# Another order for the first eleven stretches of an attention kernel, rows spread by GpSimd, and three moves in its routed path

## The chip, the cores and the metric

The kernel runs on one core of a Trainium2 chip. The metric is the device time of one execution in microseconds (us); the median of several executions is taken. The core has five engines, each with its own instruction queue: TensorE (PE, matmuls), VectorE (DVE), ScalarE (ACT), GpSimd (POOL) and SyncE (SP, which here only issues transfers). They meet through semaphores. A transfer (DMA) is issued by an engine's queue and carried out by sixteen DMA engines that all queues share.

## What is computed

The reference, cut to what matters:

```python
def reference(A_x, A_k_cache, A_v_cache, A_wq, A_wo, B_x, B_w_r, B_w_gate, B_w_up, B_w_down):
    xn = _layernorm(A_x)                        # 2048 tokens x 640
    s = _A_ref(xn, A_k_cache, A_v_cache, A_wq, A_wo)
    g = _silu(_B_ref(xn, B_w_r, B_w_gate, B_w_up, B_w_down))
    return A_x + s * g

def _A_ref(x, k_cache, v_cache, wq, wo):        # 32 heads of 192, the last 512 keys
    q = (x @ wq).reshape(B, Sq, 32, 192)
    p = _softmax(q . k * 192 ** -0.5)
    return (p . v).reshape(B, Sq, 32 * 192) @ wo

def _B_ref(x, w_r, w_gate, w_up, w_down):       # two tokens of 2048 pass an expert
    r = x @ w_r
    idx = jnp.argsort(-r)[:, :2]
    y = (_silu(x[idx] @ w_gate) * (x[idx] @ w_up)) @ w_down      # F = 1536
    return x.at[idx].add(y * _sigmoid(r[idx]))
```

The two functions are shortened here to their arithmetic. All inputs and the output are bfloat16. I call the first the attention and the second the routed path.

## The kernel before

The 2048 tokens are 16 blocks of 128. The attention works on 256 units, each two heads by one block. Four units, a pair of heads by 512 tokens, make a step (64 steps), and three units make a stretch (86 of them, the first two with two units). The kernel is software-pipelined by stretch: in stretch j PE makes the scores of its units, some q for later steps, then the product with v of stretch j - 1 and some of the output projection.

The instructions of every engine stand in the order in which the program issues them; no scheduler reorders them. Tokens write this order out, and `first` (L647) turns each into instructions. For stretches 0 to 10 the list `FIRST` (L843) is written by hand (`J0 = 11`, L842); from 11 on, `stretch(j)` (L813) makes the tokens by rule. The order of the tokens decides the order on each engine alone; engines wait for each other's results. The tokens, with n a block or unit, j a stretch, i a step:

- `x`, `k`, `v`, `wq`, `wo`: a load of tokens, keys, values or weights, on SP's queue, or on ACT's with the suffix `.a`.
- `bn` (DVE, L163) or `as` (ACT, L233 and L234, with one instruction of POOL, L235): the statistics of a block. `pw.lo.hi`: the reciprocal roots for blocks lo to hi - 1, four instructions of POOL (L211 to L214). `ap.n`: the normalization into `xn`, on ACT (`a`, L246), POOL (`g`, L249) or DVE (`v`, L251). `sx`, `ex`, `sq`, `rc`: function tables of ACT and the roots of blocks 0 and 1.
- `turn.n`: five transposes of `xn` on PE and a copy (L255). `xT.lo.hi`: the same for two blocks by a transposing DMA on SP (L262).
- `kt`: the transposes of the first pair's keys on PE (L265); `kT.p`: those of a later pair by DMA on SP (L119).
- `q.i.c`: five matmuls (L301) for a third of a step's q, and `qe.i.c` its way out of PSUM (L289 to L293), on ACT unless the token ends in `.v`; in the first step, split in two halves by two further numbers, it runs on ACT in every case.
- `S.j`: six scores of 512 keys, each of two matmuls (L315, then L322). `M.n.h`: a row maximum on DVE (L330). `E.n.h`: an exponential on ACT (L337). `P.n`: the transpose of the exponentials by DMA on SP, into `pT` (L342). `R.j`: reciprocals of the sums (L346).
- `O.n`: eight matmuls with v (L356); `OO` does two units. `Oe.n`: their scaling on DVE or ACT (L371, L369). `T.j`: the transpose of the result by DMA on SP (L377).
- `W.w`: the output projection of one block and two steps (L404); `We.w`: its way out into `s_acc` (L416, L418).
- `B.j.slot`: what the background has in stretch j, at its start (slot 0), behind the exponentials (1), in the middle (2) or at its end (3). The list of the background is written with `at(unit, slot, ...)` (L729). In the part that `FIRST` covers all of these are empty; `B.12.3` is the first of the routed path.

PSUM has eight banks: `ps_f` two ("f": q, a single `O`, the transposes), `ps_p` six ("p": scores, `OO`, the projection). A bank is handed to the next user in the order in which the former users gave theirs back.

The routed path is background work. `m_open` (L437) comes at unit 36 (stretch 12): it loads the router's row w_r onto all 128 partitions and makes constants on POOL. `m_r` (DVE) makes the router's score of each block from unit 39 on, `m_rows` and `m_top` (L476) turn them and find the two best of each block; these 64 numbers go to a buffer in DRAM (`c_d`) and come back on all partitions (L488 to L491). `m_sel` (L493), `m_tok` and `m_own` find the two best of all and gather their rows from the input by an indirect DMA; `m_norm` (L536) normalizes them, with the reciprocal root on POOL, `m_scale` and `m_xsT` follow. `m_mul` (L564) makes the expert's gate and up products of a third of F, `m_hT` turns the result, `m_down` (L602) multiplies by w_down, and its two rows go through another buffer in DRAM (`y_d`, L610 to L614) onto all partitions. `m_add` (L616) adds them to half of `xn` on POOL, from unit 147 on. `m_tanh` (L625, ACT) and `m_gate` (L629, DVE) make the silu of a block, from unit 186 on, one block every second unit.

Of the kernel before, what the change touches and what calls it, by code (L numbers as in the profile page):

```python
# [21 lines left out]
def kernel(ctx, tc, A_x, A_k_cache, A_v_cache, A_wq, A_wo, B_x, B_w_r, B_w_gate, B_w_up, B_w_down, out):  # L22
# [414 lines left out]
    def m_open():  # L437
# [6 lines left out]
        nc.gpsimd.dma_start(out=M["wr"], in_=B_w_r.partition_broadcast(P))  # L444
# [31 lines left out]
    def m_top():  # L476
# [12 lines left out]
        nc.gpsimd.dma_start(out=c_d, in_=cand)  # L489
# [412 lines left out]
```

## Time and profile before

| | before |
|---|---|
| median of 3 runs | 803.88 us |
| lowest, highest | 802.24, 804.67 us |
| the profiled execution | 803.23 us |
| its span, first to last instruction | 801.5 us |
| mean granted clock of TensorE | 0.996 |

Busy time by part of the span, in us:

| stretch of time | PE | DVE | ACT | POOL | granted clock |
|---|---|---|---|---|---|
| 0 to 7 | 5.55 | 3.25 | 2.32 | 0.55 | 1.00 |
| 7 to 17.6 | 8.39 | 8.59 | 9.49 | 1.56 | 1.00 |
| 17.6 to 24.1 | 4.42 | 6.13 | 6.43 | 2.88 | 1.00 |
| 24.1 to 70 | 43.42 | 34.16 | 35.09 | 11.23 | 0.96 |
| 70 to 780 | 709.05 | 558.04 | 425.92 | 148.60 | 1.00 |
| 780 to 801.5 | 14.72 | 15.00 | 2.78 | 9.96 | 0.94 |

All times inside an execution count from the start of its span. A group of instructions in the profile reads: line, engine, operation, output and inputs by the program's names, shape, count, busy time, mean of one. An engine's name with "q" is a queue of transfers, "PEld" the load of weights into TensorE. In brackets stands the idle time ahead of an instruction and what ended it. A list of waits reads: who waited for whom, total us, count, and longest.

### The profile page before, as it was taken

How to read it: one execution, taken by the hardware profiler on the slowest of the kernel's cores; microseconds unless marked ns; L12 is line 12 of the kernel's file. 1: busy time of each engine (PE TensorE's matmuls, PEld its weight loads, DVE VectorE, ACT ScalarE, POOL GpSimd, SP SyncE). 2: the span in 40 equal slices, each digit the busy share in tenths (PEclk: the TensorE clock that was granted, in tenths of full speed). 3: DMA queues.
4: the chain of work that ended last, by engine and by line, in shares of the span. 5: the costliest groups of instructions: out<-in, count | busy, mean ns of one | idle time of the engine just before them, and what ended most of it. 6: DMA issues, size and time to landing. Idle time of an engine off the chain costs nothing. (4 is left out here: it accounts for less than half of the span.)

```text
span 801.5 us, 15649 instructions
## 1 busy us (share of the span) xinstructions
PE 785.5 (98%) x5748; PEld 481.5 (60%) x5748; DVE 625.2 (78%) x1243; ACT 482.0 (60%) x1303; POOL 174.8 (22%) x194
## 2 busy tenths in 40 slices
PE   8899999999999999999999999999999999999996
PEld 4456556665666566666556665666566665566565
DVE  6876668989888777777777777777788887877786
ACT  7886676556655556655565556565566865565560
POOL 1330000000000000000001999920000000265954
PEclk9999999999999999999999999999999999999999
DMA  8999998789979999699997999879997889997994
GB/s 239 192 207 218 201 189 143 136 183 193 177 137 201 205 206 206 128 216 199 215 219 139 164 188 201 143 140 173 201 165 137 160 177 202 168 195 154 166 176 117
DMA packets 453389, 143.80 MB, mean 179 GB/s; under 512 B 422350, under 2 KB 452816, under 8 KB 453312
## 3 DMA queue, kind: packets, MB, share of 16 engines
q1 hardware_dynamic: 449872, 138.76, 92.8%
q0 software_dynamic: 928, 2.50, 1.1%
q10 hardware_dynamic: 2512, 1.54, 0.7%
q8 instruction: 45, 0.74, 0.4%
q14 instruction: 32, 0.26, 0.1%
...
## 5 line engine op out<-in xcount | busy, mean ns | idle before, releaser
L337 ACT ACTIVATE pexp<-sc,nm 128x512 bf16<-128x512 f32 x512 | 348.4, 696 | 292.5 <-issue 242.5
L330 DVE TENSOR_REDUCE nm<-sc 128x1 f32<-128x512 f32 x512 | 314.7, 681 | 78.7 <-PE sc L322 78.7
L301 PE MATMUL q_ps<-xnT,wq_p 128*128 128x512 bf16 (+1 forms) x975 | 226.3, 376 | 3.2 <-ACT pexp L337 0.8
L404 PE MATMUL w_ps<-wo_g,oT 128*128 128x320 bf16 x1542 | 223.2, 299 | 0.5 <-DMA oT<-o_sb 0.5
L404 PEld LDWEIGHTS <-oT 128*128 128x128 bf16 x1542 | 150.2, 98 | 71.0 <-DMA oT<-o_sb 0.8
L356 PE MATMUL o_ps<-v_sb,pT 128*128 128x192 bf16 x2048 | 185.2, 246 | 2.4 <-DMA pT<-pexp 1.3
L356 PEld LDWEIGHTS <-pT 128*128 128x128 bf16 x2048 | 170.9, 98 | 18.1 <-issue 4.9
L301 PEld LDWEIGHTS <-wq_p 128*128 128x128 bf16 x975 | 88.4, 98 | 127.1 <-issue 37.5
L371 DVE TENSOR_TENSOR o_sb<-o_ps,lsum 128x384 bf16<-128x384 f32 x239 | 131.6, 557 | 40.2 <-PE o_ps L356 22.0
L315 PE MATMUL sc<-kT,qT 128*128 128x512 bf16 x512 | 126.1, 382 | 0.9 <-DMA kT<-k_raw 0.9
L418 DVE TENSOR_TENSOR s_acc<-s_acc,w_ps 128x320 f32<-128x320 f32 x192 | 92.1, 483 | 32.2 <-PE w_ps L404 32.2
L337 ACT ACTIVATION_READ_ACCUMULATOR pexp<-sc,nm 128x1 f32 x512 | 109.8, 214 | 0.0
L293 ACT ACTIVATE qT<-q_ps 128x512 bf16<-128x512 f32 (+1 forms) x179 | 98.8, 606 | 1.3 <-PE q_ps L301 1.1
L315 PEld LDWEIGHTS <-qT 128*128 128x128 bf16 x512 | 49.0, 98 | 42.7 <-issue 2.1
L322 PE MATMUL sc<-kT,qT 64*128 64x512 bf16 x512 | 70.6, 382 | 0.0
L643 POOL TENSOR_TENSOR s_acc<-s_acc,xn 128x640 f32<-128x640 f32 x16 | 22.5, 1403 | 113.7 <-DVE s_acc L418 113.7
L322 PEld LDWEIGHTS <-qT 64*128 64x128 bf16 x512 | 18.1, 94 | 47.0 <-issue 36.8
L622 POOL TENSOR_TENSOR xn<-xn,yh 128x640 bf16<-128x640 bf16 x32 | 44.7, 1396 | 2.7
...
L644 POOL TENSOR_TENSOR s_acc<-s_acc,x_fin 128x640 f32<-128x640 f32 x16 | 22.4, 1400 | 62.5 <-DMA x_fin<-in_A_x_dram 61.5
L489 POOL DMA_DIRECT2D c_d<-cand x1 | 0.5, 547 | 155.4 <-DVE cand L487 155.4
L621 POOL TENSOR_SCALAR yh<-y_bc,oh 128x640 bf16<-128x640 bf16 x32 | 25.7, 803 | 5.0 <-DMA y_bc<-y_d 3.5
...
## 6 DMA issues: line engine op xcount, KB each, us to landing
...
pT<-pexp SPq DMA_TRANSPOSE x256, 3.7
...
```

What stands on the lines that cost most here:

```text
L293: nc.scalar.activation(out=out, in_=in_, func=ACT.Copy, scale=scale)
L301: nc.tensor.matmul(q_ps, lhsT=wq_of[g * PAIRS + pr][:, dc, c * P:(c + 1) * P], rhs=xnT[:, t5 * 4 + lo:t5 * 4 + hi, dc, :], start=(dc == 0) ...
L315: nc.tensor.matmul(sc_of[n][hh], lhsT=qT_of[i][:, 2 * hh, u * P:(u + 1) * P], rhs=kp[:, :, 2 * hh, :], start=True, stop=False)
L322: nc.tensor.matmul(sc_of[n][hh], lhsT=qT_of[i][hs, 1, u * P:(u + 1) * P], rhs=kp[hs, :, 1, :], start=False, stop=True)
L330: nc.vector.tensor_reduce(out=nm_of[j][:, c:c + 1], in_=sc_of[n][hh], axis=AX.X, op=ALU.max, negate=True)
L337: nc.scalar.activation(out=pe_of[n][:, hh, :], in_=sc_of[n][hh], func=ACT.Exp, bias=nm_of[j][:, c:c + 1], scale=1.0, accum_out=l_of[j][:, ...
L356: nc.tensor.matmul(ps[:, hh, :], lhsT=pT_of[n][:, hh, jj, :], rhs=v_sb[:, hh, jj, :], start=(jj == 0), stop=(jj == NJ - 1))
L371: nc.vector.tensor_tensor(out=osb_of[j][:, m], in0=ps, in1=l_of[j][:, 2 * m:2 * m + 2].unsqueeze(2).to_broadcast([P, 2, Dh]), op=ALU.mult)
L404: nc.tensor.matmul(w_ps, lhsT=oT_of[j][:, stretches[j].index(n), c % 3, :], rhs=wo_of[g][:, c, lo:hi], start=(c == 0), stop=(c == CPG - 1))
L418: nc.vector.tensor_tensor(out=acc, in0=acc, in1=w_ps, op=ALU.add)
L621: nc.gpsimd.tensor_scalar(out=yh, in0=M["y_bc"][:, j, :], scalar1=M["oh"][:, n, j:j + 1], scalar2=0.0, op0=ALU.mult, op1=ALU.add)
L622: nc.gpsimd.tensor_tensor(out=xn[:, n, :], in0=xn[:, n, :], in1=yh, op=ALU.add)
```

## The change

Four things are edited. The hand-written order `FIRST` is replaced: the same work in another sequence, some of it on other engines. Blocks 4 and 14 get their statistics from DVE (`bn`) instead of ACT (`as`). `kT.1` stands ahead of `P.0` and no longer behind it. The normalizations of blocks 5, 7 and 14 go to POOL, of 6 and 15 to DVE, of 8 and 12 to ACT. Five ways out of q, fifteen scalings of o and three of the projection change between DVE and ACT. One load of tokens and two of keys go to ACT's queue, and `wq.1`, `wq.2` and `k.1.0` leave it for SP's.

Three rows (w_r, the candidates, the expert's result) are no longer loaded onto 128 partitions; a short load brings each to one partition, and POOL's `partition_broadcast` spreads it. The candidates and the expert's result no longer pass through DRAM. In the built program this puts six switches of POOL's code library into its queue, one ahead of each broadcast and one ahead of the next instruction of the ordinary kind (in the lines of the new kernel L446, L457, L493, L545, L616, L620). The other switch of the program, near L142, is in both.

`m_mul` moves from slot 2 (middle) to slot 3 (end) of its stretch, and for the first third with its `m_hT` from unit 86 to unit 88, one stretch on. `m_tanh` moves from slot 1 to slot 0, `m_gate` of every even block from slot 3 to slot 2.

The diff, without the lines of `FIRST` for stretches 6 to 10:

```diff
--- before.py
+++ after.py
@@ -441,7 +441,9 @@
         M["s"] = M["stack"].enter_context(tc.tile_pool(name="moe_s", bufs=1))
         M["ws"] = (M["w"], M["s"])
         M["wr"] = M["s"].tile([P, D], BF16, name="wr_bc", tag="t3")
-        nc.gpsimd.dma_start(out=M["wr"], in_=B_w_r.partition_broadcast(P))
+        row = M["s"].tile([1, D], BF16, name="wr_row", tag="t1")
+        nc.gpsimd.dma_start(out=row, in_=B_w_r.rearrange("(o d) -> o d", o=1))
+        nc.gpsimd.partition_broadcast(M["wr"], row)
         M["r"] = M["s"].tile([P, NTB], FP32, name="r_pn")
         M["r_b"] = M["s"].tile([P, P], BF16, name="r_b", tag="turned")
         nc.gpsimd.memset(M["r_b"], 0.0)
@@ -485,10 +487,10 @@
         nc.vector.tensor_copy(out=cand[:, 0, :], in_=top[:, 0:2])
         nc.vector.tensor_copy(out=cand[:, 1, :], in_=loc[:, 0:2])
         nc.vector.tensor_scalar(out=cand[:, 1, :], in0=cand[:, 1, :], scalar1=M["base"][:, 0:1], scalar2=None, op0=ALU.add)
-        c_d = tc.dram_tile([NTB, 2, 2], FP32, name="c_d")
-        nc.gpsimd.dma_start(out=c_d, in_=cand)
+        row = M["s"].tile([1, NTB, 4], FP32, name="cand_row", tag="t2")
+        nc.gpsimd.dma_start(out=row, in_=cand.rearrange("n k c -> n (k c)"))
         M["cand"] = M["w"].tile([P, NTB, 2, 2], FP32, name="cand_bc", tag="w")
-        nc.gpsimd.dma_start(out=M["cand"].rearrange("p n k c -> p (n k c)"), in_=c_d.rearrange("n k c -> (n k c)").partition_broadcast(P))
+        nc.gpsimd.partition_broadcast(M["cand"].rearrange("p n k c -> p (n k c)"), row.rearrange("o n k -> o (n k)"))
 
     def m_sel():
 
@@ -607,11 +609,11 @@
                                  start=(fc == 0), stop=(fc == FC - 1), skip_group_check=True)
         y_sb = M["s"].tile([P, DQ], BF16, name="y_sb", tag="t2")
         nc.vector.tensor_scalar(out=y_sb, in0=y_ps, scalar1=M["sgp"][:, 0:1], scalar2=None, op0=ALU.mult)
-        y_d = tc.dram_tile([2, D], BF16, name="y_d")
+        row = M["s"].tile([1, 2, 4, DQ], BF16, name="y_row", tag="rows")
         for c in range(4):
-            nc.gpsimd.dma_start(out=y_d[:, c * DQ:(c + 1) * DQ], in_=y_sb[32 * c:32 * c + 2, :])
+            nc.gpsimd.dma_start(out=row[:, :, c, :], in_=y_sb[32 * c:32 * c + 2, :])
         M["y_bc"] = M["w"].tile([P, 2, D], BF16, name="y_bc", tag="w")
-        nc.gpsimd.dma_start(out=M["y_bc"], in_=y_d.partition_broadcast(P))
+        nc.gpsimd.partition_broadcast(M["y_bc"].rearrange("p k d -> p (k d)"), row.rearrange("o k c d -> o (k c d)"))
 
     def m_add(n):
         def f():
@@ -759,16 +761,16 @@
     for fb, n0 in enumerate((72, 91, 106)):
         for q in range(2 * DC):
             at(n0 + q, 0, m_ffn_piece(fb, q))
-        at(n0 + 14, 2, m_mul(fb))
-        at(n0 + 14, 3, m_hT(fb))
+        at(n0 + (16, 14, 14)[fb], 3, m_mul(fb))
+        at(n0 + (16, 14, 14)[fb], 3, m_hT(fb))
     for q in range(FC // 2):
         at(121 + 2 * q, 0, m_wd_piece(q))
     at(124, 3, m_sig)
     at(138, 2, m_down)
     for n in range(NTB):
         at(147 + 2 * n, 3, m_add(n))
-        at(186 + 2 * n, 1, lambda n=n: m_tanh(n))
-        at(186 + 2 * n, 3, lambda n=n: m_gate(n))
+        at(186 + 2 * n, 0, lambda n=n: m_tanh(n))
+        at(186 + 2 * n, 2 + n % 2, lambda n=n: m_gate(n))
     at(220, 3, fin_open)
 
 
@@ -841,18 +843,18 @@
 
     J0 = 11
     FIRST = """
-B.3.3 x.0.0.1.a x.0.1.2 k.0.0 bn.0.0 k.0.1.a bn.1.0 x.0.2.3 bn.0.1 sx sq.0.1 wq.0 bn.1.1 sq.1.2 kt.0.a rc.0.1 ap.0.v rc.1.2 kt.1.v x.0.3.4 ap.1.v bn.2.0 turn.0.a turn.1.v q.0.0.0.2 q.0.2.0.2 ex bn.2.1 qe.0.0.v.0.2 k.1.0.a bn.3.0 bn.3.1 qe.0.2.v.0.2 wq.1.a x.1.2.4 q.0.1.0.2 qe.0.1.a.0.2 x.1.0.2 pw.2.4 
-S.0 k.1.1 as.4 ap.2.v ap.3.v turn.2.v turn.3.a M.0.0 q.0.0.2.4 E.0.0 M.1.0 q.0.2.2.4 qe.0.0.v.2.4 E.1.0 bn.7.0 q.0.1.2.4 M.0.1 qe.0.2.v.2.4 v.1 qe.0.1.a.2.4 bn.6.0 B.2.0 bn.7.1 E.0.1 
-S.1 bn.6.1 x.2.0.2 M.1.1 q.1.2 x.2.2.4 as.5 q.1.0 pw.4.8 v.0 M.2.1 E.1.1 qe.1.2.a M.2.0 E.2.0 R.0 M.3.1 E.2.1 as.8 q.1.1 ap.6.g ap.4.v ap.5.v M.3.0 B.3.2 E.3.0 qe.1.0.v P.0 kT.1 bn.11.0 B.3.1 bn.9.0 ap.7.v O.0 qe.1.1.v E.3.1 bn.11.1 P.1 
-S.2 B.3.0 P.2 B.2.1 bn.9.1 xT.4.6 xT.6.8 M.4.0 as.10 P.3 B.4.0 M.5.0 pw.8.12 Oe.0.a M.4.1 O.1 E.5.0 M.5.1 q.2.0 E.5.1 x.3.0.2 Oe.1.v E.4.0 M.6.0 E.6.0 qe.2.0.v T.0 x.3.2.4 E.4.1 P.4 q.2.1 R.1 q.2.2 M.6.1 qe.2.1.v B.2.2 ap.8.g qe.2.2.v E.6.1 ap.9.g O.2 
-S.3 Oe.2.a ap.11.v M.7.0 P.5 M.8.0 M.8.1 as.12 ap.10.g O.3 E.7.0 Oe.3.a P.6 E.8.0 q.3.1 q.3.0 M.9.1 M.9.0 E.8.1 M.7.1 bn.13.0 E.7.1 qe.3.0.v OO.4.5 xT.8.10 R.2 E.9.0 Oe.4.v E.9.1 xT.10.12 qe.3.1.a Oe.5.v q.3.2 qe.3.2.v bn.13.1 P.8 
-S.4 T.1 O.6 as.15 B.2.3 q.4.1 B.7.2 P.7 Oe.6.a M.10.1 P.9 R.3 M.10.0 E.10.0 M.12.0 q.4.0 E.12.0 wo.0.0 M.11.0 wo.0.1 E.10.1 E.11.0 P.10 qe.4.1.v T.2 M.12.1 OO.7.8 M.11.1 E.12.1 qe.4.0.v E.11.1 O.9 Oe.7.v Oe.8.v Oe.9.v as.14 
-S.5 pw.12.16 P.11 q.4.2 M.13.0 E.13.0 M.13.1 P.12 M.14.0 M.14.1 M.15.0 E.14.0 ap.15.g B.5.3 B.4.3 E.14.1 q.5.0 qe.5.0.a E.13.1 M.15.1 qe.4.2.v W.0 B.6.3 ap.14.v E.15.0 OO.10.11 R.4 Oe.10.a E.15.1 T.3 B.5.2 Oe.11.a P.14 O.12 Oe.12.a ap.12.g P.13 We.0.v B.6.1 
...
+x.0.0.1.a x.0.1.2 bn.0.0 x.0.3.4.a bn.0.1 k.0.0 bn.1.0 B.2.0 x.0.2.3 k.0.1.a sq.0.1 wq.0 rc.0.1 sx B.3.3 bn.1.1 ap.0.v x.1.0.2 sq.1.2 rc.1.2 kt.0.a turn.0.a bn.3.0 kt.1.a bn.3.1 ap.1.v turn.1.v bn.2.0 bn.2.1 q.0.0.0.2 x.1.2.4 qe.0.0.v.0.2 q.0.2.0.2 q.0.1.0.2 v.0 qe.0.2.v.0.2 bn.4.0 qe.0.1.v.0.2 
+S.0 bn.4.1 pw.2.4 ex bn.6.0 ap.2.v k.1.0 ap.3.v M.0.0 turn.2.a turn.3.v M.0.1 q.0.0.2.4 wq.1 E.0.0 k.1.1 qe.0.0.v.2.4 q.0.2.2.4 bn.7.0 B.3.0 E.0.1 q.0.1.2.4 qe.0.2.v.2.4 x.2.2.4 bn.7.1 qe.0.1.v.2.4 bn.6.1 M.1.0 x.2.0.2 as.5 M.1.1 pw.4.8 
+S.1 B.3.1 M.2.0 q.1.2 M.3.0 B.4.0 qe.1.2.v M.2.1 v.1 q.1.1 kT.1 E.1.0 q.1.0 P.0 E.1.1 ap.4.v qe.1.1.a M.3.1 ap.6.v E.2.0 qe.1.0.v B.2.2 E.3.0 R.0 ap.5.g P.1 E.3.1 B.5.3 bn.9.0 O.0 ap.7.g E.2.1 as.8 bn.9.1 bn.11.0 Oe.0.v xT.4.6 
+S.2 M.4.0 M.6.0 bn.11.1 M.5.0 as.10 xT.6.8 P.2 E.5.0 O.1 P.3 Oe.1.v E.6.0 M.4.1 pw.8.12 q.2.0 E.4.0 M.5.1 B.3.2 B.5.2 qe.2.0.v q.2.2 x.3.0.2 x.3.2.4 E.4.1 ap.11.v E.5.1 T.0 M.6.1 P.4 qe.2.2.v R.1 q.2.1 qe.2.1.v ap.10.g bn.13.0 E.6.1 P.6 
+S.3 R.2 M.7.0 as.12 O.2 E.7.0 M.8.0 Oe.2.v ap.8.a M.7.1 O.3 Oe.3.v E.7.1 P.5 q.3.1 qe.3.1.a M.8.1 E.8.0 ap.9.g M.9.1 B.4.3 E.8.1 xT.10.12 M.9.0 T.1 q.3.0 E.9.0 q.3.2 OO.4.5 qe.3.0.v E.9.1 qe.3.2.v Oe.4.a as.15 R.3 Oe.5.v 
+S.4 O.6 xT.8.10 P.8 bn.13.1 M.10.0 P.7 Oe.6.a M.11.0 q.4.1 M.12.0 M.10.1 qe.4.1.v B.2.3 P.9 wo.0.0 E.11.0 bn.14.0 bn.14.1 E.12.0 wo.0.1 M.11.1 E.10.0 T.2 E.10.1 B.7.2 E.11.1 M.12.1 E.12.1 OO.7.8 Oe.7.v O.9 P.11 P.10 P.12 Oe.8.v Oe.9.v 
+S.5 q.4.0 pw.12.16 M.14.0 M.13.0 qe.4.0.a ap.15.v R.4 M.13.1 M.15.0 B.2.1 M.14.1 q.5.0 E.13.0 ap.14.g B.6.2 B.6.1 M.15.1 E.13.1 q.4.2 E.14.0 qe.5.0.v W.0 E.14.1 B.10.3 E.15.0 We.0.v OO.10.11 ap.13.g Oe.10.a Oe.11.a qe.4.2.v xT.14.16 E.15.1 
...
     """.split()
 
     for token in FIRST:
```

More of the change, by code (lines that the diff above doesn't have):

```diff
@@ L852 @@
-S.7 Oe.15.v qe.6.0.v M.20.0 q.6.1 B.10.3 M.19.0 M.21.0 qe.6.1.v E.19.0 B.5.1 M.21.1 M.20.1 M.19.1 E.20.0 q.6.2 E.21.0 E.19.1 E.20.1 W.3 O.18 W.4 T.5 wq.2.a v.2 qe.6.2.v E.21.1 We.4.v OO.16.17 k.3.0 R.6 We.3.a Oe.16.v Oe.17.a
-S.8 M.22.0 Oe.18.a M.23.1 E.22.0 B.9.1 P.21 M.22.1 q.7.0 R.7 M.24.1 P.19 M.23.0 P.20 E.22.1 E.23.0 B.7.0 q.7.1 qe.7.0.a k.3.1 qe.7.1.a E.23.1 W.6 M.24.0 W.5 We.6.v E.24.0 wq.3 E.24.1 OO.19.20 B.6.0 P.22 Oe.19.a T.6 We.5.v Oe.20.a B.9.0
-S.9 P.23 M.26.0 kT.3 B.10.1 M.26.1 O.21 Oe.21.v M.25.1 E.26.0 q.8.0 M.25.0 E.26.1 E.25.0 E.25.1 W.7 q.7.2 B.10.2 M.27.0 qe.8.0.a P.24 OO.22.23 E.27.0 M.27.1 qe.7.2.v E.27.1 T.7 P.26 R.8 B.8.1 Oe.22.v Oe.23.a q.8.1 P.25 kT.2 We.7.v
@@ L855 @@
-S.10 M.28.0 M.28.1 M.29.0 qe.8.1.a O.24 R.9 B.8.3 B.8.2 B.9.2 Oe.24.v P.27 E.28.0 v.3 M.30.0 E.28.1 q.9.0 qe.9.0.v E.29.0 M.30.1 E.30.0 OO.25.26 M.29.1 B.10.0 P.28 Oe.25.a q.8.2 E.29.1 B.9.3 E.30.1 O.27 qe.8.2.a Oe.26.a T.8 W.9 P.29 P.30 Oe.27.a W.8 wo.1.1 We.9.a T.9 We.8.a
+x.0.0.1.a x.0.1.2 bn.0.0 x.0.3.4.a bn.0.1 k.0.0 bn.1.0 B.2.0 x.0.2.3 k.0.1.a sq.0.1 wq.0 rc.0.1 sx B.3.3 bn.1.1 ap.0.v x.1.0.2 sq.1.2 rc.1.2 kt.0.a turn.0.a bn.3.0 kt.1.a bn.3.1 ap.1.v turn.1.v bn.2.0 bn.2.1 q.0.0.0.2 x.1.2.4 qe.0.0.v.0.2 q.0.2.0.2 q.0.1.0.2 v.0 qe.0.2.v.0.2 bn.4.0 qe.0.1.v.0.2
@@ new lines @@
+S.6 R.5 T.3 B.6.3 O.12 M.16.0 M.17.0 B.4.1 P.14 ap.12.a q.5.1 Oe.12.v B.7.3 M.17.1 P.13 E.16.0 M.16.1 E.17.0 M.18.1 E.16.1 W.2 B.8.0 qe.5.1.a xT.12.14 M.18.0 E.18.0 P.15 E.18.1 T.4 We.2.v q.5.2 E.17.1 OO.13.14 qe.5.2.v P.16 k.2.0 B.7.1 P.18 Oe.13.v Oe.14.v q.6.0 W.1 B.5.0 O.15 We.1.a qe.6.0.a
+S.7 M.21.0 P.17 Oe.15.a E.21.0 M.19.1 M.19.0 T.5 E.19.0 M.20.0 M.21.1 v.2 q.6.1 B.10.2 wo.1.0 qe.6.1.v k.2.1.a M.20.1 k.3.0.a E.19.1 B.4.2 q.6.2 E.21.1 R.6 E.20.0 W.4 P.21 We.4.a O.18 E.20.1 OO.16.17 Oe.16.v wq.2 P.19 W.3 qe.6.2.v We.3.a Oe.17.v
@@ new lines @@
+S.8 M.22.0 q.7.1 P.20 k.3.1 Oe.18.a M.24.0 E.22.0 M.23.0 M.23.1 M.22.1 E.23.0 q.7.0 E.22.1 E.23.1 W.6 qe.7.0.a M.24.1 W.5 E.24.0 B.9.0 E.24.1 OO.19.20 B.8.1 wq.3 P.23 We.6.v R.7 We.5.a Oe.19.v Oe.20.v B.9.1 P.22 B.5.1 B.10.0
+S.9 B.6.0 qe.7.1.a O.21 M.26.0 Oe.21.v M.26.1 q.8.0 E.26.0 M.25.1 q.7.2 M.25.0 E.26.1 E.25.0 qe.7.2.v E.25.1 M.27.1 M.27.0 E.27.0 W.7 E.27.1 qe.8.0.a We.7.v R.8 P.24 OO.22.23 T.6 q.8.1 Oe.22.a Oe.23.v
+S.10 M.28.1 qe.8.1.a M.28.0 E.28.0 M.29.0 q.9.0 B.7.0 kT.2 P.25 M.29.1 O.24 B.8.3 P.26 B.8.2 P.27 M.30.0 E.28.1 R.9 qe.9.0.v Oe.24.a OO.25.26 T.7 E.29.0 E.29.1 M.30.1 B.9.3 T.8 O.27 q.8.2 P.28 Oe.25.a v.3 wo.1.1 E.30.0 W.8 E.30.1 B.10.1 B.9.2 We.8.a Oe.26.v P.30 P.29 Oe.27.a T.9 qe.8.2.a W.9 kT.3 We.9.a
```

1 line of the change is left out of this document (removed).

## The prediction

> **What bounds the kernel now.** I read the engine totals first, then busy time by stretch, then what TensorE waited for, then its order of work where it waited.
>
> ```profile
> PE 785.5 (98%) x5748; PEld 481.5 (60%) x5748; DVE 625.2 (78%) x1243; ACT 482.0 (60%) x1303; POOL 174.8 (22%) x194
> ```
> ```profile
> core 0: us, PE busy (x) PEld busy (x) DVE busy (x) ACT busy (x) POOL busy (x), PEclk, DMA share, GB/s
> 7.00:10.40 3.40, 2.00 (x24) 1.58 (x22) 2.90 (x8) 2.98 (x5) 0.00 (x0) 1.00 1.09 360
> 20.70:24.10 3.40, 1.46 (x12) 0.90 (x11) 3.40 (x9) 3.37 (x9) 1.18 (x3) 1.00 1.18 142
> 24.10:27.50 3.40, 3.40 (x10) 0.95 (x11) 1.35 (x5) 2.50 (x8) 1.43 (x4) 0.51 1.24 235
> 27.50:70.00 42.50, 40.02 (x279) 22.80 (x275) 32.81 (x63) 32.59 (x91) 9.80 (x25) 1.00 1.07 204
> 70.00:780.00 710.00, 709.05 (x5223) 436.66 (x5222) 558.04 (x1098) 425.92 (x1156) 148.60 (x139) 1.00 0.96 178
> ```
>
> TensorE (PE) is busy 98% of the span. Between 70 and 780 us it idles 710.00 - 709.05 = 0.95 us. All that this change does to the routed path lies there, so no edit to it can gain more than 0.95 us; it can only lose. The loss that can be won back lies before 70 us, and there the other engines are full: from 20.7 to 24.1 VectorE (DVE) and ScalarE (ACT) were busy without a break while PE worked 1.46 of 3.40 us. Right behind it the granted clock is 0.51, once in the run.
>
> ```profile
> PE o_ps L356 <- DVE qT L291: 1.0, 1, 1.0
> PE o_ps L356 <- DMA pT<-pexp: 0.9, 2, 0.8
> ...
> PE w_ps L404 <- DMA oT<-o_sb: 0.5, 1, 0.5
> PE q_ps L301 <- DMA xnT<-xn: 0.4, 1, 0.4
> ```
> ```profile
> 17.59 3.71 PE L301 MATMUL q_ps<-xnT,wq_p 128*128 128x512 bf16 x15
> 22.33 0.82 PE L356 MATMUL o_ps<-v_sb,pT 128*128 128x192 bf16 x8 [1.03 <-DVE qT L291]
> 24.06 2.68 PE L315 MATMUL sc<-kT,qT 128*128 128x512 bf16 x6 [0.91 <-DMA kT<-k_raw]
> 26.68 1.23 PE L322 MATMUL sc<-kT,qT 64*128 64x512 bf16 x6
> 27.84 0.83 PE L356 MATMUL o_ps<-v_sb,pT 128*128 128x192 bf16 x8
> 29.48 0.81 PE L301 MATMUL q_ps<-xnT,wq_p 128*128 128x512 bf16 x3 [0.80 <-ACT pexp L337]
> ...
> 33.43 1.46 PE L315 MATMUL sc<-kT,qT 128*128 128x512 bf16 x6
> 34.82 0.82 PE L322 MATMUL sc<-kT,qT 64*128 64x512 bf16 x6
> 35.58 0.83 PE L356 MATMUL o_ps<-v_sb,pT 128*128 128x192 bf16 x8
> ...
> 71.02 2.33 PE L301 MATMUL q_ps<-xnT,wq_p 128*128 128x512 bf16 x10
> ```
>
> The first view lists waits of the first 130 us, the second PE's work in order of time, with the wait ahead of it in brackets. Three waits stand in a row: the product with v at 22.33 waited for an evacuation of q, the scores of stretch 2 at 24.06 for the transposed keys, the q of step 2 at 29.48 (the transposes of `xnT`, below). The scores of stretch 2 took 27.84 - 24.06 = 3.78 us; the same twelve matmuls of stretch 3 took 35.58 - 33.43 = 2.15. So the low clock cost 1.63 us.
>
> **The change part by part.** *The order of stretches 0 to 10.* The matmuls are the same ones; what moves is what they wait for. On the way, two blocks' statistics (`as.4`, `as.14`) go from ACT to DVE.
>
> ```profile
> 18.69 1.52 SPq L119 DMA_TRANSPOSE kT<-k_raw  x1
> ...
> 23.78 3.06 SPq L262 DMA_TRANSPOSE xnT<-xn  x2
> ```
> ```profile
> xnT<-xn SPq DMA_TRANSPOSE x6, 4.1
> ```
> ```profile
> 50.78 3.68 DVE L330 TENSOR_REDUCE nm<-sc 128x1 f32<-128x512 f32 x6 [1.06 <-PE sc L322]
> ```
> ```profile
> 12.04 0.80 DVE L251 TENSOR_SCALAR xn<-x_in,mv,rstd 128x640 bf16<-128x640 bf16 x2 [1.14 <-POOL rstd L212]
> ...
> 21.59 0.68 DVE L291 TENSOR_SCALAR qT<-q_ps 128x512 bf16<-128x512 f32 x1
> ```
> ```profile
> 16.38 0.72 ACT L337 ACTIVATE pexp<-sc,nm 128x512 bf16<-128x512 f32 x1
> ...
> 17.93 0.83 ACT L234 ACTIVATE junk_a<-x_in,nmr 128x640 bf16<-128x640 bf16 x1
> ```
> ```profile
> 19.22 1.02 POOL L212 TENSOR_TENSOR rstd<-rstd,half_m 128x4 f32<-128x4 f32 x1
> 20.32 0.20 POOL L213 TENSOR_TENSOR nmr<-mv,rstd 128x4 f32<-128x4 f32 x1
> 20.61 0.20 POOL L214 TENSOR_SCALAR nmr<-nmr 128x4 f32<-128x4 f32 x1
> ...
> 28.06 1.75 POOL L249 TENSOR_SCALAR xn<-x_in,rstd,nmr 128x640 bf16<-128x640 bf16 x2
> ```
>
> I walk the new order by queue with these durations, from the end of S.1, which I leave at 17.5 (before: 17.59). The loads and statistics ahead of it are reshuffled, but the last to come before q.0 is still the copy of block 1 on DVE; I give this part 0 and bound it by 0.5 us either way.
>
> Step 1: q.1.2, q.1.1, q.1.0 and O.0 follow without a wait, because O.0's PSUM bank was q.1.1's, which now leaves through ACT early. Ten such matmuls take 2.33 us where nothing holds them (at 71.02), 0.17 of it the last one's way out, so 15 take 3.3, and O.0 about 0.65: it ends at 21.4. S.2 needs qe.1.0 on DVE. That stands behind qe.1.2 (which can start when q.1.2 is done, 18.8), two row maxima and two normalizations: 18.8 + 0.6 + 0.6 + 0.4 + 0.6 + 0.4 + 0.6 = 22.0, a row maximum being 3.68 / 6 = 0.61. S.2 starts at 22.1 instead of 24.06; the wait of 1.03 becomes one of 0.7.
>
> Step 2: the keys' transpose stands ahead of P.0 in SP's queue and no longer behind it. Ahead of it are only loads, the last of which need block 3 normalized (12.04 + 0.80 = 12.8 before). So it is issued near 14, not 18.69; before, it landed 24.06 - 18.69 = 5.4 us later, thus now near 19.4, ahead of 22.1. The 0.91 goes.
>
> Step 3: S.2 at full clock takes 2.15, O.1 0.65: PE is free at 24.9. q.2.0 needs `xnT` of blocks 4 to 7. Their chain: `as.5` ends on ACT at 17.9 (before: 17.93 + 0.83 = 18.8; one exponential, 0.72, fewer now stands ahead of it, and S.1 ends 0.1 sooner); POOL's 0.20 + 1.02 + 0.20 + 0.20 and gaps to 19.8; the normalizations of blocks 5 and 7, now both on POOL, 1.75 to 21.5. xT.4.6 goes out at 20.8, xT.6.8 behind it (3.06 / 2 each) at 22.2, and lands 4.1 later: 26.3. Before, the second went out near 25.3. So q.2.0 starts at 26.4, not 29.48: 3.1 us earlier. PE waits 1.4 us there, and this wait is what is late next; everything that came before it in this walk is hidden by it. The six landings took 3.5 to 5.2 us, so the 3.1 is 3.7 to 2.0.
>
> Step 4: from q.2.0 to S.10 the walk meets waits of 0.27 (q.2.1 for the bank that qe.2.0 clears), 0.2 (q.3.1, Oe.2), 0.85 (O.7 and O.9 for their pT, which stand in SP's queue behind three transposes) and 0.43 (S.6 for the exponential E.15.1, put behind Oe.10 and Oe.11 on ACT): 1.75. Before, the 0.8 (pT), 0.5 and 0.4 in the list make 1.7. I count no gain here; that these waits all vanish or double gives 1.75 either way. After S.6 PE is the bound in both, so a lead at 70 us is kept.
>
> By the trace the low clock came after a stretch with 1.94 us of idle PE in 3.40, and not after 7.00 to 10.40 with 1.40. The new walk's worst 3.4 us (23.0 to 26.4) has 1.4 to 1.5, so I take the clock as granted; if it is not, 1.63 comes back. The Trainium skill ("TensorE: Matmul & The Clock Gate", Part 1: The HAM clock gate) says that the clock halves after an idle window of about 3.4 us whose phase differs from run to run, and that gaps under some 3 us are safe. The trace disagrees on the second: no gap before 24.1 exceeded 1.1 us. By the page the new order is safe too, so it leaves the sum as it is.
>
> *Rows spread by GpSimd.* Three loads that spread a row over 128 partitions become a short load, a broadcast on POOL, and six switches of POOL's code library (each broadcast one in, one out). No row shows a broadcast or a switch.
>
> ```profile
> 55.39 0.76 POOL L444 DMA_DIRECT2D wr_bc<-in_B_w_r_dram  x1
> ...
> 213.15 0.55 POOL L489 DMA_DIRECT2D c_d<-cand  x1 [155.40 <-DVE cand L487]
> ```
> ```profile
> 129.55 0.82 DVE L466 SCALAR_TENSOR_TENSOR junk<-xn,wr_bc 128x640 bf16<-128x640 bf16 x1
> ...
> 230.15 0.17 DVE L497 COPY val<-cand_bc 128x32 f32<-128x32 f32 x1
> ```
> ```profile
> c_d<-cand POOLq DMA_DIRECT2D x1, 0.2 KB, 3.1
> ```
> ```profile
> L627 ACT ACTIVATE tz<-xn x16: 772/778/782, 576.5 to 668.7; 128x640 f32<-128x640 bf16 x16
> ```
>
> The router's row is issued at 55.39 and read at 129.55. The candidates go out at 213.15 and are read at 230.15: 17.0 us, less 3.1 for the short load leaves 13.9 for a switch and a broadcast. The last row, the result's, feeds POOL's additions, which nothing reads before tanh at 576.5; POOL is idle between. Lower end 0. Upper end, with the cover gone: DVE stands at L497, behind it the scalings of o and the row maxima, then PE; each us beyond 13.9 costs one. The nearest instructions are POOL's over 128x640, 0.20 to 1.75 for two, far under 13.9, so I take 0. The Trainium skill ("GPSIMD Engine Reference", 2.1 Instruction dispatch) gives about 6 us for the first call into freshly loaded code; no run here shows it yet. By it the row is there at 213.15 + 3.1 + 6 + 1, still ahead of 230.15, and the sum stays.
>
> *Tanh, gate, expert product.* The 16 tanh (0.78) go from the end of a stretch to its start, ahead of the exponentials, where ACT waits for the row maxima; the gates of even blocks from the end to the middle on DVE; the three products from the middle to the end of a stretch, the first also one stretch on. PE work is unchanged. Against: at most 0.78 us in a stretch, or 1.56 where two fall together, ahead of P and so of the next stretch's o; that is hidden as long as pT lands a stretch ahead. I take 0; bounds -0.95 (all of the idle) and +1.56 once.
>
> **Sum.** The profiled execution took 803.23, its span 801.5. 803.23 - 3.1 = 800.1. The median of the runs is 803.88, 0.65 above it; from there 800.8. I take the middle, 800.4.
>
> **The rivals.**
> (a) The low clock comes back at the 1.4 us wait. For it: 1.46 of 3.40 busy was enough before, and the new window is near 1.95. Gain 3.1 - 1.6 = 1.5 from the same middle, 803.55: 802.1.
> (b) The order runs with few waits, Step 3's wait and half of Step 4's gone: 3.1 + 1.4 + 0.9 = 5.4: 798.2. For it: my walk takes each transfer at its median. Against: POOL's two normalizations are serial.
> (c) The order does not do what the walk says: SP issues as many transposes in the same time, and its queue stays the limit before 60 us, so the early lead is waited away at pT. 803.5.
> (d) Slower: switch and broadcast of the candidates take over 13.9 us. Place: DVE at L497, about 230. At 21 us the loss is 7.1, net 4.0: 807.6. It decides from 13.9; from 13.9 + 3.1 = 17.0 the kernel is slower than before. Or the six switches, each bringing code in, delay the transposes that land then: at 1 us of PE each it is 800.4 + 6 = 806.4. Against: an idle POOL, and nothing near that long in its rows.
>
> **How the numbers follow.** About 0.3% (2.4 us) is what a measurement of this kernel can tell from no change: the bounds are 801.5 and 806.3. Forecast 0.47, of which 0.38 falls under 801.5 and 0.09 above; (a) 0.12; (b) 0.18; (c) 0.08; (d), with any other loss of that size, 0.15. Faster 0.38 + 0.18 + 0.02 of (a) = 0.58; slower 0.15; the rest 0.27. The range is from (b) less 0.4 for a slow part in the first 17 us that may also go, 797.8, to (c) plus the spread of the runs above their median, 0.8, 804.3; it leaves out (d) and some of (b). The likeliest case alone, with landings of 3.5 to 5.2 us, is 799.4 to 801.9.
>
> **What would show it.** Step 1 and 3: S.2 near 22.1, q.2.0 near 26.4 and waiting for `xnT`. Step 2: no wait for `kT`. Clock: no row under 1.00 between 10 and 70. Step 4: from S.7 on, PE's work some 3 us earlier than before. Rows: DVE without a wait ahead of its copy of the candidates. Wrong: PE idle over 1.5 us between 70 and 780, or q.2.0 after 28.

## The result and the profile after

| | before | changed |
|---|---|---|
| median | 804.96 us (22 runs) | 803.11 us (22 runs) |
| lowest, highest | 802.24, 807.58 us | 801.6, 805.41 us |
| the profiled execution | 803.23 us, span 801.5 | 805.41 us, span 803.6 |

The ratio is 0.9977, with a 95% interval of 0.9967 to 0.9988: the changed kernel is 1.85 us faster. Two later sets of runs, of 9 and of 12, gave 0.9971 [0.9958, 0.9983] and 0.9981 [0.9962, 0.9999]. The time lies in the range that was given, but the gain is little more than half of the 3.5 us forecast.

The profiled execution of the changed kernel is the slowest of its 22 runs, that of before lies under its median. So a difference between these two executions is not yet one between the kernels, and below each segment is read from several profiles. First, what TensorE waited for in the first 130 us after the change:

```profile
PE tp_k L273 <- DMA k_raw<-in_A_k_cache_dram: 3.5, 1, 3.5
PE q_ps L301 <- DMA xnT<-xn: 2.8, 2, 1.6
...
PE o_ps L356 <- DMA pT<-pexp: 0.6, 1, 0.6
PE o_ps L356 <- ACT pexp L337: 0.5, 1, 0.5
PE sc L315 <- ACT pexp L337: 0.3, 1, 0.3
```

The kT wait of before and the q wait (qT) are gone. New is a wait of 3.5 us for the first keys, in the part that the prediction had set at nothing. TensorE's work in order of time, from S.1 on:

```profile
19.24 1.22 PE L315 MATMUL sc<-kT,qT 128*128 128x512 bf16 x4
...
24.91 0.83 PE L356 MATMUL o_ps<-v_sb,pT 128*128 128x192 bf16 x8 [0.57 <-DMA pT<-pexp]
25.58 1.46 PE L315 MATMUL sc<-kT,qT 128*128 128x512 bf16 x6
...
29.81 3.62 PE L301 MATMUL q_ps<-xnT,wq_p 128*128 128x512 bf16 x15 [1.25 <-DMA xnT<-xn]
33.27 1.46 PE L315 MATMUL sc<-kT,qT 128*128 128x512 bf16 x6
...
43.59 0.83 PE L356 MATMUL o_ps<-v_sb,pT 128*128 128x192 bf16 x8
46.01 1.25 PE L301 MATMUL q_ps<-xnT,wq_p 128*128 128x512 bf16 x5 [1.59 <-DMA xnT<-xn]
47.75 3.77 PE L356 MATMUL o_ps<-v_sb,pT 128*128 128x192 bf16 x24 [0.48 <-ACT pexp L337]
```

S.1 starts 3.4 us later than before, q.2.0 (at 29.81) only 0.3 us later. Then q.4.1 waits 1.59 us for `xnT`, and 24 matmuls with v take 3.77 us. The same work by stretches of time, with the granted clock behind the five engines:

```profile
7.00:10.40 3.40, 1.04 (x11) 1.05 (x12) 1.12 (x4) 0.29 (x1) 0.00 (x0) 1.00 1.07 364
20.70:24.10 3.40, 3.40 (x19) 1.39 (x15) 3.28 (x7) 2.96 (x8) 2.28 (x6) 1.00 1.17 149
24.10:27.50 3.40, 2.83 (x22) 1.38 (x20) 3.30 (x10) 3.37 (x11) 1.60 (x3) 1.00 0.99 191
26.40:29.80 3.40, 2.16 (x17) 0.94 (x16) 3.30 (x8) 3.30 (x9) 0.38 (x2) 1.00 1.12 209
44.20:47.60 3.40, 1.48 (x8) 0.41 (x5) 1.84 (x4) 2.03 (x6) 0.00 (x0) 1.00 0.69 151
47.60:51.00 3.40, 3.25 (x21) 3.08 (x22) 3.37 (x8) 2.95 (x10) 1.57 (x4) 0.52 0.94 215
70.00:780.00 710.00, 708.89 (x5226) 437.06 (x5225) 555.79 (x1093) 425.76 (x1151) 147.93 (x138) 1.00 0.96 177
```

Two things are to be seen. The half clock is not gone; it stands at 47.6 to 51, right behind the 1.59 us wait. And from 70 to 780 TensorE idles 710.00 - 708.89 = 1.11 us, against 0.95 before.

Subtracting the starts of stretches (the first score matmul of each, as at 19.24 or 33.27 above) gives a table in which the segments can be compared between executions (us):

| segment | before, 2 profiles | changed, 3 profiles |
|---|---|---|
| start of S.1 | 15.89, 17.27 | 19.24, 18.85, 17.82 |
| S.1 to S.3 | 17.54, 17.34 | 14.03, 13.99, 14.15 |
| S.3 to S.7 | 35.45, 35.08 | 38.29, 38.38, 37.57 |
| S.7 to S.11 | 38.27, 38.77 | 37.96, 37.96, 37.87 |
| S.13 to S.44 | 283.07, 283.15 | 283.16, 282.91, 283.03 |
| S.44 to S.61 | 153.90, 155.31 | 154.20, 154.24, 154.99 |
| S.61 to S.74 | 119.45, 119.44 | 118.82, 118.84, 118.84 |
| S.74 to S.85 | 95.30, 95.31 | 95.31, 95.31, 95.31 |

The new order takes 3.4 us less from S.1 to S.3 and some 2.8 more from S.3 to S.7. In both, 0.66 us is neither won nor lost: the new list has one product with v, `O.2`, behind S.3 and no longer ahead of it. TensorE's order of time at S.3, in before (S.3 at 33.43), then changed (S.3 at 33.27):

```profile
32.77 0.82 PE L356 MATMUL o_ps<-v_sb,pT 128*128 128x192 bf16 x8
```
```profile
35.41 1.49 PE L356 MATMUL o_ps<-v_sb,pT 128*128 128x192 bf16 x16
```

So the lead at S.3 is 2.7 us, and 2.2 of it are gone at S.7, where the walk had no change. Some 0.6 us are won from S.7 to S.11, and 0.62 from S.61 to S.74, where only the routed path was edited. From S.1 to S.11 the changed kernel took 90.1 us in the mean, before 91.2. One later place spreads as much as all this: S.44 to S.61 took 153.1 to 155.3 us over all profiles of the study, in waits for pT and for q near 413 to 424 us that come and go within one kernel.

### The profile page after: what moved, and what is told of

It is laid out like the page before. It is cut to its first block, busy times and chain, and to the rows that moved or that the text cites. A ratio compares the mean times of both kernels' runs of the same rounds, so it can differ in the third digit from the quotient of the medians.

```text
span 803.6 us, 15640 instructions
## 1 busy us (share of the span) xinstructions
PE 785.5 (98%) x5748; PEld 483.7 (60%) x5748; DVE 625.7 (78%) x1247; ACT 479.9 (60%) x1291; POOL 175.4 (22%) x192
## 4 chain that ended last, share of the span: by engine, by line
PE 71%; DMA 1%; DVE 1%; issue 0%; ACT 0%; DVEq 0%
PE w_ps L404 20%; PE q_ps L301 19%; PE o_ps L356 16%; PE sc L315 10%; PE sc L322 6%; DMA pT<-pexp 1%; PE gu_ps L571 0%; DVE fin_t L423 0%; DVE fin_o L425 0%; ACT pexp L337 0%; DVE o_sb L371 0%; PE y_ps L608 0%; PE tp_o L389 0%; DVE lsum L346 0%; DVEq L425 0%
## 5 line engine op out<-in xcount | busy, mean ns | idle before, releaser
L371 DVE TENSOR_TENSOR o_sb<-o_ps,lsum 128x384 bf16<-128x384 f32 x246 | 135.6, 556 | 41.3 <-PE o_ps L356 22.1
L614 POOL DMA_DIRECT2D y_row<-y_sb x4 | 2.3, 572 | 172.7 <-DVE y_sb L611 172.7
```

The lines of the kernel that those rows point to most:

```text
L371: nc.vector.tensor_tensor(out=osb_of[j][:, m], in0=ps, in1=l_of[j][:, 2 * m:2 * m + 2].unsqueeze(2).to_broadcast([P, 2, Dh]), op=ALU.mult)
```

## The experiments

**The changed kernel again.**

> The changed kernel again, beside the next three. Theory A (the start): the 3.5 us that TensorE waited for the first keys comes from the order of the early loads, so a second profile shows a wait of 2 us or more at the same place, and S.1 ends near 20.9 and not 17.6. Theory B (chance): that one execution was unlucky; a second profile shows under 1 us there. Ratio to before 0.997 to 0.999 either way.

Measured 0.9971; the wait for keys was 2.7 us, S.1 started at 18.85. By these two profiles Theory A; the third had 2.1 and 17.82:

> The changed kernel once more, as the measure for the two beside it. Ratio 0.997 to 0.998; S.3 to S.7 takes 38.3 us, S.11 to S.13 15.85 us; S.1 starts between 17 and 19.3.

Measured 0.9981 [0.9962, 0.9999]; S.3 to S.7 took 37.57, without the half clock of the other two there.

**The new list alone, and everything but the list.** `FIRST` of the changed kernel put into the kernel before, and the reverse.

> The kernel before with the new list for stretches 0 to 10 and nothing else of the change. Theory A: the whole of the gain is here, ratio 0.9977 within 0.001, the routed path being covered. Rival (the routed path gives some back): without its edits the gain is larger, near the forecast 0.9957.

> The changed kernel with the old list for stretches 0 to 10: broadcasts, tanh, gate and product alone. Theory A: 1.000 within 0.001; from 70 us on, TensorE idles less than 1.2 us. Rival (the routed path gives some back): 1.001 to 1.003.

The list alone: 0.9994 [0.9975, 1.0013]. The rest alone: 0.9989 [0.9977, 1.0001]. Neither came as forecast: the list alone was to bring the whole gain or more, and brings nothing that can be told from zero; the rest, counted at nothing, comes out no smaller, and cannot be told from zero either. (TensorE's idle time between 70 and 780 us was to stay under 1.2 us with the rest alone; it was 1.66.) In the list's profile S.1 to S.3 took 14.50 us, and the start of S.3 lay 3.1 us ahead of that in the first profile of before. From S.3 to S.7 2.1 us of this went, `O.2` among it, and 1.7 from S.11 to S.13. The second loss, in the order of time on TensorE:

```profile
113.76 1.03 PE L315 MATMUL sc<-kT,qT 128*128 128x512 bf16 x4
116.28 0.61 PE L315 MATMUL sc<-kT,qT 128*128 128x512 bf16 x2 [1.50 <-DMA kT<-k_raw]
```

The new list puts the keys of the fourth pair (`kT.3`) last in stretch 10, and S.12 is the first to need them. The changed kernel has them at the same place and did not wait: there this transfer landed 3.8 us after its issue, here 5.6.

**The second head's keys first.**

```diff
-x.0.0.1.a x.0.1.2 bn.0.0 x.0.3.4.a bn.0.1 k.0.0 ... k.0.1.a sq.0.1
+x.0.0.1.a x.0.1.2 bn.0.0 bn.0.1 k.0.0 ... k.0.1.a x.0.3.4.a sq.0.1
```

> The changed kernel, but on ScalarE's queue the second head's keys are loaded ahead of block 3 and no longer behind it. Theory A: the wait for the first keys falls from 3.5 to under 1 us, S.1 ends near 18, and the time falls by some 2 us against the changed kernel, to a ratio near 0.995. Rival (the bytes ahead decide, not their order on the queue): the wait stays over 2 us, no gain. Second rival: the wait goes, but block 3, now later, holds up stretch 1 by as much.

Measured 802.56 us, 0.9967 [0.9955, 0.9979], against 0.9971 for the changed kernel beside it: no difference that the intervals show. In this profile nothing waited for keys, and S.1 started at 17.34; the 2 us that were expected did not come. But over all profiles of the study the mean start of S.1 was 16.70 us with the old loads (six, 15.21 to 18.81), 18.13 with the new ones (seven, 15.79 to 19.24) and 17.73 with the keys first (seven, 16.25 to 18.50). The edit explains little of it, and the spread of one kind, over 3 us even on one chip, is wider than the difference; the second profile of before shows why one execution says little:

> The kernel before, a second profile. Theory A (the order of the early loads): the keys' transposes on TensorE wait under 1 us again and S.1 starts within 1 us of 15.9, against 18.9 to 19.2 in two profiles of the changed kernel. Theory B (chance): S.1 starts anywhere between 15.8 and 19.2. Either way the low clock stands once before 70 us, and the first stretches differ from the first profile by more than the 710 us behind them.

```profile
10.20:13.60 3.40, 3.40 (x19) 2.04 (x19) 1.63 (x5) 1.66 (x4) 1.30 (x4) 0.69 0.79 218
23.80:27.20 3.40, 2.43 (x14) 1.19 (x12) 2.83 (x8) 3.37 (x10) 1.06 (x2) 0.81 1.19 168
```

These stretches of time are from the same program as the first profile of before. S.1 started at 17.27, the keys were waited for 1.0 us, and the clock fell twice, at other places; the execution took 806.08 us.

**The transposes of blocks 8 and 9 ahead of T.1.** In stretch 3, `... xT.10.12 M.9.0 xT.8.10 T.1`, and no longer `S.4 O.6 xT.8.10`.

> The changed kernel, but on SP's queue the transposes of blocks 8 and 9 stand ahead of T.1 and no longer behind it. Theory (step 4 was mis-sized by this wait and the low clock behind it): the wait for xnT near 46 us falls from 1.6 to under 0.5, no low clock at 47 to 51, and the time falls by 1.5 to 3 us against the changed kernel, to a ratio near 0.995. Rival (the next wait takes it): the pT behind T.1 come as late, ratio 0.997.

Measured 0.9979 [0.9963, 0.9996]. TensorE's order of time:

```profile
44.04 1.24 PE L301 MATMUL q_ps<-xnT,wq_p 128*128 128x512 bf16 x5
47.92 3.81 PE L356 MATMUL o_ps<-v_sb,pT 128*128 128x192 bf16 x24 [2.64 <-DMA pT<-pexp]
```

q.4.1 no longer waits, and the next product waits 2.64 us for `pT` in its place, with the half clock behind it as before. S.3 to S.7 took 38.72 us. The rival holds: what was moved forward on SP's queue pushed the rest back.

**Both, and the fourth pair's keys.** `kT.3` from the end of stretch 10 to behind `T.8`.

> Both corrections: the second head's keys ahead of block 3, and the transposes of blocks 8 and 9 ahead of T.1. If the two losses are independent their gains add: some 2 and some 2 us under the changed kernel, a ratio near 0.993. Rival (a later wait caps the lead, above all the keys' transposes kT of the fourth pair, which in the changed kernel landed 0.6 us ahead of their use): TensorE waits for kT near 113 us, and the ratio stays near 0.996.

> The kernel before this one, but with the fourth pair's keys transposed behind T.8 and no longer as the last of stretch 10. If kT caps the lead: no wait for kT, and 1 to 1.5 us less than without this edit. If it doesn't: the same time within 0.5 us, and the three transposes of P now behind it may cost up to 1.5 us at the next products with v.

Measured 0.9969 [0.9953, 0.9986] and 0.9974 [0.9956, 0.9992]: neither apart from the changed kernel. S.3 to S.7 took 36.92 and 38.31 us, so two executions with the same order there differ by 1.4; TensorE idled 2.5 us in both, and only the second had the half clock there. Neither waited for kT, the one with the old place included; whether kT caps a lead is not told by this pair.

**Four loads off SP's queue.** `x.3.0.2`, `x.3.2.4`, `wo.0.0` and `wo.0.1` on GpSimd's queue. The first two also move forward, to the start of stretch 2; they were issued from 27.37 on and not from 30.45.

> The changed kernel, with four loads (the last block group's tokens at the start of stretch 2, wo of the first group in stretch 4) on GpSimd's queue and no longer among the transposes on SP's. Theory C (SP's queue, busy 94% from 19 to 58 us, sets the pace of the first stretches, so what is won before 33 us is waited away behind it): 2.25 us leave that queue, the waits for xnT and pT between 44 and 50 us shrink by 1 us or more in sum, the way from S.3 to S.7 takes 1 to 2 us less than the 38.3 us of two profiles, and the ratio comes near 0.995. Theory D (the wait is for the engines that make the rows, ACT and POOL): S.3 to S.7 stays at 38 us and the ratio at 0.997.

> The four loads moved as in the kernel before this one, and the second head's keys loaded ahead of block 3. Theory C: the gain of the earlier start is kept, since SP's queue has room: S.7 starts near 67.5, against 68.8 with the keys alone; ratio near 0.994. Theory D: as with the keys alone, 0.9967.

Measured 1.0038 [1.002, 1.0056] and 1.0039 [1.0013, 1.0065]: slower, as neither theory said. TensorE waited 6.61 us for pT in one place of the first profile and 5.08 in the second. These are transfers of 26 to 60 us, in the changed kernel and in the first of the two:

```profile
wo_g<-in_A_wo_dram SPq DMA_DIRECT2D x2, 480.0 KB, 4.8
x_in<-in_A_x_dram SPq DMA_DIRECT2D x2, 320.0 KB, 4.0
...
oT<-o_sb SPq DMA_TRANSPOSE x4, 4.0
```
```profile
wo_g<-in_A_wo_dram POOLq DMA_DIRECT2D x2, 480.0 KB, 9.0
x_in<-in_A_x_dram POOLq DMA_DIRECT2D x2, 320.0 KB, 6.0
...
oT<-o_sb SPq DMA_TRANSPOSE x3, 6.5
```

The last number is the median time from issue to landing. The same loads from the other queue took 4.2 and 2.0 us longer, and the transposes of o 2.5 us. The medians of the other transposes hardly moved (pT 3.5 against 3.3 us), but the two of P that were issued at 44.78 and 46.22, beside the loads of wo, took 9.1 and 9.6 us. ACT's exponentials waited for pT as well (ACT's waits, 26 to 60 us):

```profile
ACT pexp L337 <- DMA pT<-pexp: 6.7, 2, 4.1
```

The bytes were the same, so the room on SP's queue alone did not help. What the earlier place of the two loads of x did by itself was not tried.

**One transfer fewer.** Blocks 8 and 9 turned by TensorE: `R.3 Oe.5.v turn.9.v turn.8.v S.4`, without `xT.8.10`.

> The changed kernel, with blocks 8 and 9 of xn turned by TensorE at the end of stretch 3 (ten transposes, two copies on DVE) and no longer by a DMA on SP in stretch 4. Theory C2 (between 24 and 60 us transfers set the pace, the share of the DMA engines standing at 1.0 to 1.2 there, so only less transferring helps): the wait for xnT near 46 us goes, no wait of over 1 us takes its place, and S.3 to S.7 takes 36 to 37 us, not 38.3, although TensorE works 0.74 us more; ratio near 0.995. Theory F (the rows come too late from ACT, which makes exponentials and statistics there without a break): the next product with v waits as long for pT, S.3 to S.7 stays at 38 us or more.

> The same with the second head's keys ahead of block 3. Theory C2: the two gains add to a ratio near 0.994. Theory F: 0.997.

> Keys first and blocks 8 and 9 turned by TensorE, again: S.3 to S.7 takes 36.1 us, S.11 to S.13 17.0 us with a wait of 1 us for kT, as in its first profile. Under the changed kernel by 1 to 2 us.

S.3 to S.7 took 36.10, 36.10 and 36.31 us, against 37.57 to 38.38 in the changed kernel and 37.47 with the keys first, although TensorE works 0.74 us more. TensorE's order of time in the first of them:

```profile
42.47 0.83 PE L356 MATMUL o_ps<-v_sb,pT 128*128 128x192 bf16 x8
43.14 1.24 PE L301 MATMUL q_ps<-xnT,wq_p 128*128 128x512 bf16 x5
44.80 2.15 PE L356 MATMUL o_ps<-v_sb,pT 128*128 128x192 bf16 x24 [0.41 <-ACT pexp L337]
...
113.45 1.03 PE L315 MATMUL sc<-kT,qT 128*128 128x512 bf16 x4
115.59 0.61 PE L315 MATMUL sc<-kT,qT 128*128 128x512 bf16 x2 [1.12 <-DMA kT<-k_raw]
```

The wait of 1.59 us and the half clock behind it are gone (24 matmuls take 2.15 us again, not 3.77), and the wait of 0.41 us at 44.80 is all that stands in their place. So transfers set the pace there, as C2 said, and not ACT; whether by their turn on SP's queue or by the DMA engines behind it, these runs do not separate. But a wait for kT stands at 115: S.11 to S.13 takes 17.14 us, not 15.84. In runs nothing of this is seen: 1.0005 [0.9993, 1.0017] alone and 0.9976 [0.9964, 0.9988] with the keys first (801.55 us), where 0.995 and 0.994 were expected; later 0.9983 [0.9964, 1.0001], beside 0.9981 of the changed kernel, where 1 to 2 us less were expected.

> The kernel beside it with the fourth pair's keys transposed behind T.8. Theory G (the wait for kT caps any lead won before): S.11 to S.13 falls to 15.85 us, and the time by some 1 us. Rival: the transposes of P behind it come late instead, S.11 to S.13 stays at 16.5 us or more. Best kernel of the study if G holds: ratio near 0.996 on this chip.

With `kT.3` behind `T.8`, S.11 to S.13 fell from 17.04 to 16.19 us: the wait for kT is gone, and 0.17 us of wait for pT came. That it caps a lead, as Theory G has it, is not shown. Four of the five profiles with this wait reach S.11 earlier than all without it, by 106.2 us, but the one with the transposes of blocks 8 and 9 ahead of T.1 reached it at 109.6, no earlier than the changed kernel, and waited 1.4 us for kT too. In all five the transfer took 5.5 to 5.6 us from issue to landing, and 3.8 in those with the same place and no wait; what makes it longer stays open. Ratio 0.9971 [0.9956, 0.9986], 802.48 us. No kernel of the study is shown to beat the changed one: all the better ratios lie within its intervals.

**The gain at the tanh.** The moved gates alone, the moved tanh alone, and both.

> The kernel before, with the gates of even blocks in the middle of their stretch, and nothing else of the change. Theory E (the 0.64 us that every kernel with the moved tanh and gate wins between stretches 61 and 74 is the gate's: two gates in a row no longer stand ahead of the row maxima on DVE): S.61 to S.74 takes 118.8 us, not 119.45. Rival (it is the tanh's place on ACT): 119.45. One time, so no ratio is read from it.

> The kernel before with the tanh at the start of their stretch, and nothing else. The gates alone lost 7 us; so either the 0.64 us between stretches 61 and 74 need both moves (this kernel: 119.4 to 119.5 us from S.61 to S.74), or the tanh alone brings them (118.8 us). One time, so no ratio is read from it.

> The kernel before with both moves, tanh to the start and the gates of even blocks to the middle, and no broadcast and no other order: if the 0.64 us are theirs, S.61 to S.74 takes 118.8 us; if they need the broadcasts, 119.45. One time, so no ratio is read from it.

S.61 to S.74 took 126.18, 119.50 and 118.73 us. So the 0.62 us are the two moves' together; the gate alone makes DVE wait for a tanh that comes late, in six stretches (DVE's waits, 600 to 690 us):

```profile
DVE xn L630 <- ACT tz L627: 12.3, 6, 2.4
```

DVE's order of time around S.65, which starts at 597.63 in before and at 599.79 with both moves, says where they win:

```profile
598.31 1.55 DVE L630 SCALAR_TENSOR_TENSOR xn<-tz,xn 128x640 bf16<-128x640 f32 x2
599.77 3.67 DVE L330 TENSOR_REDUCE nm<-sc 128x1 f32<-128x512 f32 x6
```
```profile
600.47 0.82 DVE L630 SCALAR_TENSOR_TENSOR xn<-tz,xn 128x640 bf16<-128x640 f32 x1
601.61 3.68 DVE L330 TENSOR_REDUCE nm<-sc 128x1 f32<-128x512 f32 x6 [0.32 <-PE sc L322]
```

Before, two gates stood in a row ahead of the row maxima, which began 2.14 us after the scores; with one gate they begin after 1.82, and wait for the scores. S.65 takes 9.00 us, not 9.24. How the maxima come to hold TensorE was not followed further; in before its q at 603.82 waited (0.08 us) for ACT's copy of an earlier one.

## Why the prediction fell short

**Steps 1 to 3 were right, seen from S.1 on.** S.2 came 25.58 - 19.24 = 6.34 us after S.1 (before: 24.06 - 15.89 = 8.17), without a wait for kT. From S.1's end, 20.93, q.2.0 came 29.81 - 20.93 = 8.9 us later; the walk had 26.4 - 17.5 = 8.9. It waited 1.25 us for `xnT`, against 1.4. One wait stood elsewhere: Step 1 had O.0 without one and S.2 waiting 0.7 us for q; O.0 waited 0.57 us for pT, and S.2 not at all. That the two are nearly equal is luck.

**Step 4 failed: "I count no gain here", with the lead "kept".** The walk met waits of 1.75 us and took them as equal to the old ones. In the first profile 2.4 us of wait (1.59, 0.48, 0.29) came, and the half clock with them; in the third 3.1 us came without it; the two of before idled 1.7 and 1.4 us there. For the same work S.3 to S.7 took 2.2 us more than before in the mean (2.8 with `O.2`). The walk did see pT "behind three transposes" in SP's queue, but set no price on the transposes of blocks 8 and 9. In before they left at 37.13, in the changed kernel behind others:

```profile
40.44 1.38 SPq L262 DMA_TRANSPOSE xnT<-xn  x1
```

They landed 5.5 us later, at 45.97 (5.1 and 5.2 us in the other two profiles), where the walk takes 4.1. S.7 came at 71.56, not some 3 us ahead of 68.88; q.2.0 after 28, the prediction's own sign of being wrong, came by the late start. Rival (c), that transfers stay the limit and the lead is waited away, was given 0.08 and is the nearest to what happened: moving a transpose forward only moved the wait, taking one away won 1.4 to 2.3 us of this segment. Its end, 803.5 from a middle of 803.55, still left out what the other parts won; that the runs came near it is luck.

**The start was taken as 0, with 0.5 either way.** By the profiles the mean start of S.1 is 1.4 us later with the new loads, and executions with the same loads spread over 3.6. The walk began at the copy of block 1 and did not look at the keys, issued second on ACT's queue before (1.20) and third now (1.67). That their place is the cause is not shown; putting them back took away 0.4 of the 1.4.

**The clock was taken as granted, and priced too high.** Rival (a) put its return at the wait ahead of q.2.0. In the changed kernel this is 26.4 to 29.8, with 2.16 of 3.40 busy and full clock. The low clock returned in two of three profiles at 47.6, behind 1.48 of 3.40. The 1.63 us that the prediction set on it are the price of the matmuls, not of the stretch: of six profiles with the old list, the two of before have the low clock ahead of the wait for q.2.0 and take 17.54 and 17.34 us from S.1 to S.3; three have none and take 17.38, 17.23 and 16.83, because this wait is then 2.05 to 2.26 us and not 0.80 and 0.62. In the sixth the low clock came behind the wait, and the way took 19.07. From S.3 to S.7 the changed kernel took 38.3 and 38.4 us with it and 37.6 without. In the Trainium skill ("TensorE: Matmul & The Clock Gate", Part 1: The HAM clock gate) the window of activity runs free of the program; two profiles of before with the clock down at 10.2 in one and not in the other agree. Its advice to keep gaps under some 3 us was not enough here: no gap in the 30 us ahead of these two returns exceeded 1.64 us.

**The broadcasts cost nothing, as said, and the cover held.** POOL and DVE after the change:

```profile
215.84 0.71 POOL L491 DMA_DIRECT2D cand_row<-cand  x1 [146.69 <-DVE cand L489]
222.97 0.37 POOL L493 PARTITION_BROADCAST cand_bc<-cand_row  x1 [6.42 <-ACT qT L293]
```
```profile
232.61 0.17 DVE L499 COPY val<-cand_bc 128x32 f32<-128x32 f32 x1
```

The candidates are there at 223.3, 9.3 us early, so rival (d) was far off. The new operations have prices now: broadcasts of 0.37 to 0.93 us, and an idle POOL ahead of the first instruction behind a switch, 5.9 to 6.4 us ahead of the three broadcasts, in which the short load lands too, and 7.2 and 7.5 us on two of the ways back. The Trainium skill ("GPSIMD Engine Reference", 2.1 Instruction dispatch) had about 6 us for a first call into freshly loaded code; the trace is near it ahead of the broadcasts and 1.2 to 1.5 us above it on the ways back.

**Tanh and gate, taken as 0, won 0.62 us.** It lay inside the bound of 0.95, and the direction was open. But the bound does not bind as it was read: by the same reading TensorE idled only 0.24 us from S.61 to S.74 in before, and 0.62 were won there. The working priced ACT alone; the view above shows DVE's order to be what differs. The product cost nothing that shows: S.29 to S.31 took 19.32 us in both, and S.13 to S.44 the same within the spread.

**What stays open.** The runs do not tell why S.1 starts late or early, nor what makes a transposing transfer take 5.5 us in place of 3.5 to 3.8. The profiled executions of the changed kernel and of before end at the same time in the mean (S.85 at 776.2 and 776.1), while the runs differ by 1.5 to 2.3 us. Two of the three profiled executions of the changed kernel were its slowest, 805.41 and 804.9. Which segment is shorter in the runs without a profile cannot be read from profiles.
